# Seventeen attention blocks on GpSimd, and a shorter road for keys, queries, gate and output

## The chip, the cores and the metric

The kernel runs on one core of a Trainium2 chip. The core has five engines that work side by side and meet at semaphores: TensorE (PE, matrix products into PSUM), VectorE (DVE), ScalarE (ACT), GpSimd (POOL, which cannot reach PSUM) and SyncE (SP, which issues the transfers). The metric is the time on the device in microseconds (us). Each engine carries out its instructions in the order in which they stand in the program.

## The reference

Two attention layers over the same input x (2048 rows of 512, bf16) are mixed by a gate. Layer A is full attention over 32 heads of 16 columns. Layer B lets each position see eight earlier ones, two apart.

```
x = A_x
g = sigmoid((x * gate_w).sum(-1, keepdims=True))
a = softmax(q k^T * 16**-0.5) v  for 32 heads, then @ A_wo      # q, k, v = x @ A_wqkv
b = the same with B's weights, for keys at s, s-2, ..., s-14     # then @ B_wo
return g * a + (1 - g) * b
```

## The kernel before, in words

Layer A's scores are 32 heads x 16 tiles of 128 keys x 4 chunks of 512 queries: 2048 blocks of 128 keys by 512 queries. They are worked off in 32 periods; a period is one chunk of queries and one group of four heads (64 blocks). For a block PE multiplies a key tile and a query tile of 32 rows (a head's 16 rows and 16 rows for its bound), the exponential is taken, and PE multiplies the result by the values into one accumulator of the period (`pv_mm`); a column of constants beside the values gives the denominators.

The exponential of most blocks is ACT's: two PSUM rings, `rA` of three blocks and `rB` of two, take turns, and one ACT instruction does a ring's filling (`ex`, tile `pT`; the group pT<-ring). The others are DVE's, chosen per period by `n_dve`, 196 in all: `dq` on PE adds an offset (a matmul of `off` with the tile of ones) to the scores in a PSUM bank `misc`, and four DVE passes (`p1` to `p4`, tiles `dt` and `pd`) form the bits of a bf16 number that is the exponential.

Scores are kept in range by a bound. For each group of heads the largest absolute key entry is found (`km`, one pass over the projected keys; `kc` is a second pass that writes the keys and constant rows into `kt_all`), `selk` makes a row `rowq` of it, and the query tile `qt` carries absolute values of the query in its extra rows: `mg` masks the sign bits in PSUM and `ev` scales and writes. The first group's keys are written by ACT.

Layer B goes by tiles of 128 positions, one about every 47 us (`b_start`, `b_space`). Its keys and values are written to DRAM and read back shifted (`ksh`, `vsh`, eight shifts each); POOL multiplies and sums them (tile `prod`, two halves of logits and two of values), DVE and ACT do the small softmax, and `sm_div` multiplies by the reciprocal sums. POOL also scales A's transposed accumulators by the reciprocal denominators (`po2m`, tile `ott`).

The output of a tile is A's rows times A_wo (`a_part`), scaled by the gate on DVE (`a_ev`), and B's rows times B_wo (`b_part`), scaled by one minus the gate and added (`b_ev`). For the last two chunks the last group of heads comes separately (`tail`, `t_ev`). The gate goes through DRAM to be turned into one column per tile (`zfin`, `ztr`, `zsig`, `zgate`).

The order of all this is made when the program is built: every piece is an `Op` with an engine, a planned duration, a due time, its inputs and its buffers, and `list_schedule` places them on the engines. It also puts filler matmuls on zeros (`zero`) where PE would have too little to do. `CFG` holds planned durations, leads and the counts per period. The order on each engine is then fixed: at run time an instruction that waits holds all behind it on its engine. Nearly all instructions are issued by one helper line, so in the profile the tile names tell them apart.

At the start SP loads the four parts of x and the weights of A (x, keys, x, x, x, queries, values, 512 KB each), PE transposes x (`pxt`), and POOL and DVE copy each head's weights twice (`wtw`).

## Time and profile before

| | |
|---|---|
| median of three runs | 877.5 us (877.01 to 882.39) |
| profiled execution: its own time | 877.7 us |
| its span, first to last instruction | 875.9 us |
| mean granted clock of TensorE | 0.987 |
| busy: PE, DVE, ACT, POOL | 795.0, 735.4, 852.1, 619.3 us |
| first and last exponential of layer A | start 18.44, end 867.07 us |
| last work of layer B on POOL | end 788.7 us |
| data moved | 47.37 MB |

A row of the profile names the line, the engine and the operation, then the tiles (output <- inputs), the shapes and the count; behind the first bar are the busy time in us and the mean of one in ns, behind the second the engine's idle time just before these instructions and what ended it. A row of the timeline begins with the start and the duration, merged over instructions of one kind that follow one another.

### The profile page before, as it was taken

What the parts mean: (1) busy time and instruction counts of PE and PEld (TensorE: products, weight loads), DVE (VectorE), ACT (ScalarE), POOL (GpSimd) and SP (SyncE); (2) the same over time, 40 slices, a digit from 0 to 9 for tenths busy, and PEclk for the clock granted to TensorE, in tenths of its full rate; (3) what the DMA queues carried; (4) which work ended last, traced back from release to release, by engine and by line L of the source; (5) the groups of instructions that cost most, each with busy time, mean ns of one, the idle gap of its engine ahead of it and who ended that gap; (6) DMA issues with size and microseconds to landing.
All of it is one profiled execution on the core that took longest, in us unless ns stands there. A gap on an engine that the chain in (4) does not pass through costs nothing.

```text
span 875.9 us, 18559 instructions
## 1 busy us (share of the span) xinstructions
PE 795.0 (91%) x7468; PEld 257.9 (29%) x7468; DVE 735.4 (84%) x1217; ACT 852.1 (97%) x767; POOL 619.3 (71%) x607
## 2 busy tenths in 40 slices
PE   8999899999899999999899988899889889999885
PEld 4233233223322333223232322222222222322221
DVE  6488888898899788976869899988988998798996
ACT  5999999999999999999999999999999999999995
POOL 4176939696969779978996883979998959480000
PEclk9999999999999999999999999999999999999998
DMA  9301112103013103023120111121112031000001
GB/s 286 114 2 63 47 45 66 61 1 110 1 61 97 34 29 109 2 56 114 50 80 26 49 55 61 49 61 61 49 52 59 13 97 49 1 1 1 1 1 49
DMA packets 43998, 47.37 MB, mean 54 GB/s; under 512 B 1876, under 2 KB 41348, under 8 KB 43912
## 3 DMA queue, kind: packets, MB, share of 16 engines
q1 hardware_dynamic: 43912, 46.19, 16.6%
q8 instruction: 58, 0.95, 0.4%
q14 instruction: 28, 0.23, 0.1%
HBM read 39.86 MB, written 6.33 MB: 53 GB/s over the span
## 4 chain that ended last, share of the span: by engine, by line
ACT 66%; issue 25%; PE 7%; DVE 1%; DMA 1%; DVEq 0%; ACTq 0%
ACT pT L288 65%; PE misc_ps L300 3%; PE ring L300 2%; PE acc L300 2%; ACT lg L288 1%; DMA z_scr<-zrow 1%; PE pxt L496 1%; PE misc L300 0%; DVE zrow L288 0%; DVE osb L288 0%; ACT kt_all L288 0%; DVEq L1176 0%; DVE misc_ps L288 0%; DVE qt L288 0%; DVE accT L288 0%
## 5 line engine op out<-in xcount | busy, mean ns | idle before, releaser
L288 ACT ACTIVATE pT<-ring 128x1536 bf16<-128x1536 f32 x741 | 843.0, 1393 | 6.4 <-PE ring L300 6.1
L300 PE MATMUL ring<-qt,kt_all 32*128 32x512 bf16 x1852 | 295.9, 383 | 70.4 <-ACT pT L288 62.5
L288 POOL TENSOR_TENSOR prod<-prod 128x512 f32<-128x512 f32 (+1 forms) x208 | 240.0, 1169 | 6.3
L300 PE MATMUL acc<-pT,vp_all 128*17 128x512 bf16 (+1 forms) x1852 | 239.3, 387 | 1.0 <-ACT pT L288 0.7
L300 PEld LDWEIGHTS <-kt_all 32*128 32x128 bf16 x2048 | 119.1, 91 | 354.3 <-issue 334.8
L288 POOL TENSOR_TENSOR prod<-ksh,qb 128x512 f32<-128x512 bf16 x128 | 144.0, 1158 | 38.5 <-DMA ksh<-kv_scr 34.6
L288 DVE TENSOR_SCALAR dt<-misc 128x512 f32<-128x512 uint16 x196 | 133.9, 683 | 44.4 <-PE misc L300 42.6
L288 POOL TENSOR_TENSOR prod<-vsh,lg 128x512 f32<-128x512 bf16 x128 | 136.7, 1102 | 2.5 <-DMA vsh<-kv_scr 0.5
L288 DVE TENSOR_TENSOR dt<-misc,dt 128x512 f32<-128x512 uint16 x196 | 134.1, 684 | 4.8
L288 DVE SCALAR_TENSOR_TENSOR dt<-misc,dt 128x512 f32<-128x512 uint16 x196 | 134.2, 684 | 4.0
L288 DVE TENSOR_TENSOR pd<-misc,dt 128x512 uint16<-128x512 f32 x196 | 133.6, 681 | 2.8
L300 PEld LDWEIGHTS <-vp_all 128*17 128x17 bf16 (+1 forms) x2048 | 52.2, 88 | 127.5 <-issue 119.4
L300 PE MATMUL misc_ps<-xT,wtw 128*32 128x512 bf16 x1024 | 82.8, 384 | 0.0
L300 PE MATMUL misc<-ones_t,off 32*128 32x512 bf16 x196 | 74.9, 382 | 0.2 <-DVE osb L288 0.2
L300 PE MATMUL misc<-qt,kt_all 32*128 32x512 bf16 x196 | 73.8, 376 | 0.0
L300 PE MATMUL misc_ps<-bw,xT 128*32 128x512 bf16 x768 | 67.6, 391 | 0.0
L300 PE MATMUL acc<-ones_t,z 128*32 128x512 bf16 x179 | 63.7, 392 | 0.0
L288 POOL TENSOR_TENSOR ott<-accT,rden 128x256 bf16<-128x256 f32 x30 | 18.7, 623 | 57.1 <-DVE rden L288 57.1
L288 POOL TENSOR_TENSOR lg<-lg,mx 128x256 f32<-128x256 f32 x16 | 10.1, 631 | 48.4 <-DVE mx L288 48.4
L300 PEld LDWEIGHTS <-xT 128*32 128x32 bf16 (+1 forms) x1088 | 34.8, 96 | 28.8 <-issue 18.8
L300 PE MATMUL acc<-pd,vp_all 128*17 128x512 bf16 x196 | 42.3, 383 | 0.0
L288 POOL TENSOR_TENSOR lg<-lg,rr 128x256 f32<-128x256 f32 x16 | 10.1, 630 | 36.8 <-DVE rr L288 22.7
(73 smaller groups left out, 491.8 us busy)
## 6 DMA issues: line engine op xcount, KB each, us to landing
ksh<-kv_scr SPq DMA_DIRECT2D x16, 1024.0 KB, 6.0
vsh<-kv_scr SPq DMA_DIRECT2D x16, 1024.0 KB, 6.1
kv_scr<-kvs SPq DMA_DIRECT2D x16, 256.0 KB, 2.1
xld<-in_A_x_dram SPq DMA_DIRECT2D x4, 512.0 KB, 7.7
out_dram<-osb SPq DMA_DIRECT2D x16, 128.0 KB, 1.7
bw<-in_B_wqkv_dram SPq DMA_DIRECT2D x1, 1536.0 KB
wraw<-in_A_wqkv_dram SPq DMA_DIRECT2D x2, 512.0 KB, 8.7
wv<-in_A_wqkv_dram SPq DMA_DIRECT2D x1, 512.0 KB, 9.1
```

The costliest lines, as they stand in the source:

```text
L288: return chain_on(key, f(*a, **k))
L300: return chain(nc.tensor.matmul(out, lhsT=lhsT, rhs=rhs, start=start, stop=stop, **kw))
L496: chain(nc.tensor.transpose(out=st[half][:, c, tt * 128:(tt + 1) * 128], in_=xld[sc][:, tt, (2 * half + c) * 128:(2 * half + c + 1) * 128] ...
```

## The change

It has these parts:

- **Blocks.** The last key tiles' blocks go 202 to DVE and 17 to POOL (`n_dve`, `n_gp`). For a POOL block PE makes the scores as for DVE, DVE copies them to SBUF (into a `kvs` buffer), and POOL evaluates the same cubic in six passes (`gp_block`) with the `prod` buffer as scratch. ACT keeps 1829.
- **Keys.** For all groups but the first one DVE pass writes the projected keys and their maximum (both signs, since the extra rows hold the negated keys); `selk` joins the two, and four transfers then copy the constant rows over the extra rows from group 0.
- **Queries.** The scaling writes `qt` first, and the mask works on `qt` in SBUF, 32 bits at a time. The shift of the exponents moves into the bias of the exponential and into the offset.
- **Gate and output.** The gate is multiplied into A's reciprocal denominators and one minus the gate into B's reciprocal sums, both on POOL, so both products of an output tile are summed in one PSUM bank and DVE only copies.
- **Start.** x comes first, its first part in two halves; of the key and query weights the first four heads' columns come ahead, the rest last. Transposes go by pairs of row tiles, and DVE makes both of the first weight copies.
- **Ones.** The tile of ones shrinks to 128 columns, and matmuls that stream it read one column 512 times.
- The planning constants change. (In the first lines below they stand together; in the code each has its own line.)

```diff
-    n_dve=(3, 4, 5, 8, 4, 6, 5, 6, 7, 5, 5, 4, 6, 5, 5, 6, 8, 5, 7, 7, 7, 6, 8, 7, 7, 8, 7, 7, 8, 6, 7, 7),
-    dve_tiles=2,
+    n_dve=(4, 4, 8, 8, 3, 6, 5, 6, 5, 6, 6, 5, 5, 6, 8, 4, 9, 4, 6, 7, 7, 7, 7, 9, 6, 7, 9, 7, 7, 6, 7, 8),
+    n_gp=(1, 1, 1, 0, 0, 1, 0, 0, 0, 0, 0, 0, 1, 0, 1, 0, 0, 0, 0, 1, 1, 1, 0, 0, 0, 1, 0, 0, 2, 2, 1, 2),
+    gp_dl=8,
+    gp_lead=24,
+    dve_tiles=3,
...
-    d_slack=0.5, d_lead=4.0, dq_early=8.0, pd_bufs=5, same=3.0, early=0.25, a_slack=0.8, v_slack=0.3,
-    g_slack=2, unit=0.459, t0=18.5, b_start=30.0, b_space=46.7
+    d_slack=0.3, d_lead=3.0, dq_early=12.0, pd_bufs=4, same=3.5, early=0.3, a_slack=1.0, v_slack=0.1,
+    g_slack=3, unit=0.455, t0=17.0, b_start=32.0, b_space=47.1
...
+    def ones(rows):
+        b = ones_t[rows, 0:1]
+        return _ap(b, [list(b.ap[0]), [0, QW]])
...
+    o_x0 = load(load_x(0, 0, TPC // 2), alloc=[xtok[0]])
+    o_x[0] = load(load_x(0, TPC // 2, TPC), use=[xtok[0]])
+    o_wkh = load(load_w(1, 0, HC), alloc=[wtok])
+    o_x[1] = load(load_x(1), alloc=[xtok[1]])
+    o_x[2] = load(load_x(2), alloc=[xtok[2]])
+    o_x[3] = load(load_x(3), alloc=[xtok[3]])
+    o_wqh = load(load_w(0, 0, HC), use=[wtok])
+    o_wv = load(load_w(2))
+    o_wk = load(load_w(1, HC, D), use=[wtok])
+    o_wq = load(load_w(0, HC, D), use=[wtok])
     o_two = {}
-    o_two[1, 0] = op("dve", 0.72, twice(1, 0, 4), -6.0, deps=[o_wk], use=[wtok])
-    o_two[0, 0] = op("pool", 1.0, twice(0, 0, 4), -6.0, deps=[o_wq], use=[wtok], lat=1.3, slack=0.3)
-    o_two[1, 1] = op("pool", 5.0, twice(1, 4, H), -5.0, deps=[o_wk, o_two[0, 0]], use=[wtok], slack=1.0)
-    o_two[0, 1] = op("pool", 5.0, twice(0, 4, H), -4.0, deps=[o_two[1, 1]], use=[wtok], slack=1.0)
-    o_bw = op("sp", 1.0, load_bw, -8.3, lat=19.0)
+    o_two[1, 0] = op("dve", 0.45, twice(1, 0, 4), -6.0, deps=[o_wkh], use=[wtok])
+    o_two[0, 0] = op("dve", 0.45, twice(0, 0, 4), -5.9, deps=[o_wqh], use=[wtok])
+    o_two[1, 1] = op("pool", 3.6, twice(1, 4, H), -5.0, deps=[o_wk], use=[wtok], slack=1.0)
+    o_two[0, 1] = op("pool", 3.6, twice(0, 4, H), -4.0, deps=[o_wq], use=[wtok], slack=1.0)
...
-            V.tensor_scalar(out=kt_all[:, i, sc * QW:(sc + 1) * QW], in0=st["pk"][:], scalar1=rowc[:, 0:1],
-                            scalar2=rowc[:, 1:2], op0=ALU.mult, op1=ALU.add)
+            V.tensor_tensor_reduce(out=kt_all[:, i, sc * QW:(sc + 1) * QW], in0=st["pk"][:], in1=ones(slice(0, 128)),
+                                   scale=sign[:, 0:1], scalar=0.0, op0=ALU.mult, op1=ALU.max, accum_out=kmax_all[:, i, sc:sc + 1])
...
-        c = op("dve", 0.81, kc, dl - 0.8, deps=[b], use=[tk])
-        return op("dve", 0.70, km, dl, deps=[b, c], use=[tk])
+        return op("dve", 0.75, kc, dl, deps=[b, o_init_d], use=[tk])
...
+            if i == 0:
+                V.tensor_reduce(out=kmax[:, 0:1], in_=kmax_all[:, 0, :], axis=AX.X, op=ALU.max)
+            else:
+                V.tensor_reduce(out=kside[:, 0:1], in_=kmax_all[:, i, :], axis=AX.X, op=ALU.max)
+                V.stream_shuffle(out=kside[:, 1:2], in_=kside[:, 0:1], mask=[(p + DH) % 32 for p in range(32)])
+                V.tensor_tensor(out=kmax[:, i:i + 1], in0=kside[:, 0:1], in1=kside[:, 1:2], op=ALU.max)
...
+        def rows():
+            for j in range(4):
+                r_ = slice(32 * j + DH, 32 * j + 32)
+                SP.dma_start(out=kt_all[r_, i, :], in_=kt_all[r_, 0, :])
+        if i:
+            o_kc[i] = [op("sp", 2.2, rows, dl, deps=o_kc[i] + o_kc0, lat=6.0)] * NC
...
+        def ev():
+            V.tensor_scalar(out=qt_tiles[pi][:], in0=st["p1"][:], scalar1=rowq[:, i:i + 1], scalar2=None, op0=ALU.mult)
+
         def mg():
-            bits = st["p1"][:].bitcast(U32)
+            bits = qt_tiles[pi][:].bitcast(U32)
...
+        c = op("dve", 0.72, ev, dl - 0.8, deps=[b, o_selk[i]], use=[tk, tq])
+        o_q[pi] = op("dve", 0.35, mg, dl, deps=[c], use=[tq])
...
+    def zfin2():
+        st_g["zblk"] = work.tile([128, BPC, 32], FP32, name="zblk", tag="accT", bufs=2)
+        for j in range(4):
+            SP.dma_start(out=st_g["zblk"][32 * j:32 * j + 32, 0:2, :], in_=z_scr.rearrange("(h b p) -> b h p", b=32, p=32))
+
+    def zblk():
+        zb = st_g["zblk"][:, 0:2, :].rearrange("p h n -> p (h n)")
+        V.transpose(out=g_rows[:].rearrange("p h n -> p (h n)"), in_=zb)
+
+    def zblke():
+        A.activation(out=g_rows[:], in_=g_rows[:], func=ACT.Exp, scale=-1.0)
+
+    def zblkg():
+        V.tensor_scalar_add(out=g_rows[:], in0=g_rows[:], scalar1=1.0)
+        V.reciprocal(out=g_rows[:], in_=g_rows[:])
...
+            G.tensor_scalar(out=st["rr"][:], in0=st["rr"][:], scalar1=omg[:, t:t + 1], scalar2=None, op0=ALU.mult)
...
-            A.activation(out=st["p"][:, 0:n, :], in_=st["r"][:, 0:n, :], func=ACT.Exp, scale=LN2 / BITS)
+            A.activation(out=st["p"][:, 0:n, :], in_=st["r"][:, 0:n, :], func=ACT.Exp, scale=LN2 / BITS, bias=lift[:])
...
+        def gp_block(t, j, dl):
+            st = {}
+            tx, td, tp = tok("misc", NB), tok("kvs", 2), tok("pg", 2)
+
+            def dq():
+                st["x"] = ps.tile([128, QW], FP32, tag=f"misc{bank[0]}", bufs=1, name="misc")
+                st["xs"] = work.tile([128, 2 * D], BF16, name="kvs", tag="kvs", bufs=2)[:].bitcast(FP32)
+                row = slice(32 * j, 32 * j + 32)
+                mm(st["x"][:], off[row, :], ones(row), True, False, tile_position=(32 * j, 0))
+                mm(st["x"][:], kt_all[row, i, t * 128:(t + 1) * 128], qt_tiles[pi][row, :], False, True, tile_position=(32 * j, 0))
+
+            def cp():
+                V.tensor_copy(out=st["xs"], in_=st["x"][:])
+
+            def poly():
+                fr = st["xs"].bitcast(U16).rearrange("p (n two) -> p n two", two=2)[:, :, 0]
+                st["pd"] = work.tile([128, QW], BF16, name="pg", tag="pg", bufs=2)
+                prod = work.tile([128, WH, D], FP32, name="prod", tag="prod", bufs=1)
+                u, v = prod[:, 0, :], prod[:, 1, :]
+                G.tensor_scalar(out=u, in0=fr, scalar1=CUB_S, scalar2=None, op0=ALU.add)
+                G.tensor_tensor(out=v, in0=u, in1=u, op=ALU.mult)
+                G.tensor_scalar(out=v, in0=v, scalar1=EXP_C, scalar2=CUB_P, op0=ALU.mult, op1=ALU.add)
+                G.tensor_tensor(out=v, in0=v, in1=u, op=ALU.mult)
+                G.tensor_tensor(out=v, in0=v, in1=st["xs"], op=ALU.add)
+                G.tensor_scalar(out=st["pd"][:].bitcast(U16), in0=v, scalar1=CUB_Q, scalar2=None, op0=ALU.add)
+            a = op("pe", 0.43, dq, dl - 3.0 - cfg["gp_lead"], rows=True, deps=[o_q[pi], o_kc[i][t // TPC] if i else o_kc0[t // TPC]],
+                   alloc=[tx, td], use=[q_tok[pi]], rel=lo, lat=0.68, name=f"dq{pi}")
+            a = op("dve", 0.70, cp, dl - 2.0 - cfg["gp_lead"], deps=[a], use=[tx, td])
+            a = op("pool", 5.6, poly, dl - cfg["gp_dl"], deps=[a], alloc=[tp], use=[td], lat=5.9, slack=1.0, name=f"gp{pi}")
+            blocks.append((st, tp, a))
...
+            (gp_block if dorder.index((t, j)) >= n_dve[pi] else block)(t, j, hi - 1.0 - 3.5 * (n - 1 - q_))
...
+            E_ = V if pi >= NP - 2 else G
+            E_.tensor_tensor(out=rden[:], in0=rden[:], in1=g_rows[:, c_ // 2, (c_ % 2) * BPC:(c_ % 2 + 1) * BPC], op=ALU.mult)
...
+                    cols = slice(tt * 128, (tt + 1) * 128)
+                    if k < ng:
+                        mm_ct(st["pf"], oat_tiles[c_][:, k, cols], wop[:, k, :], k == 0, False)
+                    else:
+                        mm_ct(st["pf"], obt_tiles[c_][:, k - ng, cols], bwo[:, k - ng, :], False, k == ng + DC - 1)
...
+                V.tensor_copy(out=st["fa"], in_=st["pf"][:])
...
+                V.tensor_copy(out=st["o"][:], in_=st["pf"][:])
...
-                V.scalar_tensor_tensor(out=st["o"][:, 0:D], in0=st["pt"][:], scalar=g_sp[:, t:t + 1], in1=st["fa"],
-                                       op0=ALU.mult, op1=ALU.add)
+                V.tensor_tensor(out=st["o"][:, 0:D], in0=st["pt"][:], in1=st["fa"], op=ALU.add)
```

## The prediction

> **What bounds the kernel now.** I read the page's engine totals first, then the ScalarE (ACT) rows in order of time, then the clock row and the waits of GpSimd (POOL).
>
> ```profile
> PE 795.0 (91%) x7468; PEld 257.9 (29%) x7468; DVE 735.4 (84%) x1217; ACT 852.1 (97%) x767; POOL 619.3 (71%) x607
> ...
> L288 ACT ACTIVATE pT<-ring 128x1536 bf16<-128x1536 f32 x741 | 843.0, 1393 | 6.4 <-PE ring L300 6.1
> L300 PE MATMUL ring<-qt,kt_all 32*128 32x512 bf16 x1852 | 295.9, 383 | 70.4 <-ACT pT L288 62.5
> ```
>
> ACT is busy 97%, nearly all with one thing, the exponentials of 1852 score blocks; and it is TensorE (PE) that waits for ACT, 62.5 us, while ACT waits 6.1 us for PE. So the kernel is ACT's chain of exponentials, with something in front of it and something behind it. Those ends are in the timeline:
>
> ```profile
> 16.10 0.78 ACT L288 ACTIVATE kt_all<-misc_ps,rowc 128x512 bf16<-128x512 f32 x1 [0.52 <-DVE kmax_all L288]
> 18.44 6.88 ACT L288 ACTIVATE pT<-ring 128x1536 bf16<-128x1536 f32 x6 [1.56 <-PE ring L300]
> 25.71 1.45 ACT L288 ACTIVATE pT<-ring 128x1536 bf16<-128x1536 f32 x1 [0.39 <-PE ring L300]
> 27.52 14.71 ACT L288 ACTIVATE pT<-ring 128x1024 bf16<-128x1024 f32 x13 [0.36 <-PE ring L300]
> 43.59 4.62 ACT L288 ACTIVATE pT<-ring 128x1536 bf16<-128x1536 f32 x4 [1.35 <-PE ring L300]
> ```
> ```profile
> 849.09 17.98 ACT L288 ACTIVATE pT<-ring 128x1024 bf16<-128x1024 f32 x16
> ```
>
> The first exponential starts at 18.44. The last row is 16 of them back to back, eight of two blocks and eight of three: 40 blocks in 17.98 us, **0.4495 us per block**, ending at 867.07. The span is 875.9, so the tail is 8.8. Between 18.44 and 867.07 lie 848.6 us: 1852 x 0.4495 = 832.5, the 16 small softmax exponentials of block B 9.2, the gate's 0.2, and 6.7 lost. Of the lost time 4.5 stands in the bracketed waits of 0.36 to 1.35. Three of these waits (1.07 at 112.09, 0.57 at 376.02, 0.76 at 572.80) fall in the only stretches where the granted clock dips after the start (0.66 in 108 to 113, 0.56 and 0.76 in 368 to 378, 0.70 in 568 to 573); the 32x512 matmuls last 0.61 to 0.63 us there, elsewhere about 0.38. A dip costs ACT 0.8 us on average.
>
> **The change, part by part.**
>
> *Blocks off ACT.* VectorE (DVE) blocks go from 196 to 202, GpSimd gets 17: 1829 blocks stay on ACT, 23 fewer, 23 x 0.4495 = **10.3 us off the chain**. This counts in full as long as ACT stays the engine that everyone waits for. The exponential gets its bias from a tile in place of a constant: taken at nothing, since it reads a bias per partition either way.
>
> *What it puts on DVE.* Six blocks of four passes at 0.683: 6 x 4 x 0.683 = 16.4. Seventeen PSUM-to-SBUF copies for GpSimd, like the row that casts kvs (0.687): 11.7. Selecting a key bound gets a shuffle and a maximum on one column, near the 0.15 of the kmax row, seven times: 2.1. Gate rows and the second weight copy: 1.4. Together 31.6.
>
> *What it takes from DVE.* Keys and bounds in one pass: 28 x (0.804 + 0.681) become 28 of one pass with a second input and a maximum. No such instruction is in the trace; it costs between one 0.681 pass and the two passes it replaces, 1.485. I take 0.75, nearest the single-pass rows of this shape (0.681 to 0.804): 20.6 saved (bounds 0 to 22.5). The query mask moves from 512 words in PSUM (0.751) to 256 words in SBUF: between the 0.237 of a 16-wide SBUF reciprocal and 0.751, I take 0.4, the obt copy's 0.410: 32 x 0.35 = 11.2. The query scaling loses one of its scalars: 0.803 to 0.75, 1.7. Output: eight tiles drop 0.740 + 0.747 for one 0.687 copy, eight drop 0.751 + 0.750 for 0.69, and eight last sums 0.744 for 0.68: 6.4 + 6.5 + 0.5. Together 46.9. DVE's total falls by some 15 to 720 us, 83% of a shorter span; with the key pass at 1.485 it rises by 5. Neither makes it the bound.
>
> *GpSimd.* A block there is three two-input passes over 512 floats at 1.270 (row prod<-prod 128x512) and three one-input passes. One-input passes of that width are not in the trace: between 0.64, interpolated from the wtw copies (0.400 for 256 elements, 1.686 for 1792), and 1.270. I take 0.64, a one-input row: 5.7 us a block (upper bound 7.6), 97 for 17 (130). With 46 small multiplications at about 0.2 (between 0.10 for a one-column memset and 0.43 for 128 columns) POOL rises from 619 to some 725. Its windows: 76 of 80 us busy in 600 to 680, 56 to 71 in the other stretches between 40 and 760, and 20 of 108 after 760. The ten blocks of periods 0 to 25 add 57 us to about 590 in 740; the seven of periods 28 to 31 fall after 750, where POOL is nearly idle. So it fits on average.
>
> ```profile
> POOL ott L288 <- DVE rden L288: 57.1, 7, 25.4
> POOL lg L288 <- DVE mx L288: 48.4, 6, 10.4
> POOL prod L288 <- DMA ksh<-kv_scr: 34.6, 4, 19.8
> ```
>
> These are the places where POOL waits for others today, 140 us in all, and can absorb work.
>
> *PE.* A block taken off ACT needs one more matmul (the offset): 23 x 0.38 at most, 9 us, beside 62.5 of ring waits and 64 of filler matmuls. The offset and filler matmuls now read one repeated column of ones. No row shows such an operand; they run at 0.382 and 0.392, and the slowest row of this width, in the cold clock, is 0.63: bounds 0 to 0.25 on about 400 matmuls. I take 0, since the existing rows hardly differ with what is streamed (0.376 to 0.395).
>
> *SP and DMA.* Each head group but the first gets four transfers of 64 KB that restore the constant key rows, 28 issues in all, in SP's order between block B's loads. Issues take 0.3 to 1.0 and a 256 KB store of kvs lands in 2.1, the eight 64 KB wop loads in 8.5 beside other loads. The first scores of a group now wait for them. Behind a waiting `rows` transfer on SP stand the ksh and vsh loads and the stores; their reader is POOL, then far later the output. It is due some 19 us before its period, so I take nothing; if that cover is gone, the lateness comes on ACT once per group, seven times.
>
> *Start.* Today the sixth 512 KB load (wq) is ready at 12.55 and the first (x) at 5.01: 1.5 us each, so x's last part comes at about 11.0. In the new order a 64 KB slice of wk takes the place of all of wk ahead of it, so it comes between 9.7 and 11.0 (the slice's short rows could cost as much as the full load). From there, by rows: transposes 1.07, copy 1.01, key projection 1.05, bound 0.69, selection 0.45, query scaling 0.75, mask 0.4, scores and the first exponential 0.5, with semaphore gaps some 6.2. From PE's start at 10.4 that is 16.6, 1.9 earlier than 18.44. Bounds: 0.3 (only the mask's share: 0.6 us of it stands ahead of the selection today) to 2.2. I take **1.6**, for a slice that is a little slow.
>
> *Tail.* One multiplication of 0.2 is added in front of the last transposes; four final sums drop from 0.744 to 0.68. **0.** The new gate-row exponential is 0.2 on ACT.
>
> *Sum.* 875.9 - 10.3 - 1.6 + 0.2 = 864.2, with the 6.7 lost on ACT kept. The profiled execution took 877.7 for a span of 875.9, so 866.0; its time is 0.2 above the median of the runs shown, 877.5, so **865.8**.
>
> **A rule weighed.** The moved mask is one-source, SBUF to SBUF. The nearest DVE row of that kind beside a busy POOL, the oat transpose, lasts 698 to 711 ns at all 16 occurrences, so no blocking shows there. The Trainium skill, "SBUF — State Buffer", Who interferes with whom, says that such an operation in a two-port mode and a GpSimd instruction block each other wholly; it names scalar operations for it and not transposes, so no run here shows it. By it the mask would wait out a POOL instruction.
>
> **The rivals.**
>
> 1. *ACT's waits go.* For: DVE is relieved and the order is new. Against: the start and the clock dips made most of them. With 1 us left of 6.7 and the best start: 859.5. Chance 12%.
>
> 2. *More waits on ACT*, from clock dips or late key rows: at 0.8 a dip, or seven late groups at 1 us, 5 to 10 us: 869 to 876. For: three dips exist now with the fillers. Against: PE's load hardly changes. 10%.
>
> 3. *The mask waits for GpSimd.* POOL is busy about 76% of 40 to 760 in pieces of about 1.2 us, so a blocked mask waits 0.76 x 0.6 = 0.46 on average, at most 1.27. If this reached ACT in full, 32 x 0.46 = 15 us: 881; if half, 873. Against: the mask runs well ahead of its period, and DVE has 140 us of idle time. It eats the whole gain from 0.37 us per mask. 7%. (The skill's rule above is the ground for it.)
>
> 4. *GpSimd becomes the gate: slower.* The PV matmul of a GpSimd block sits in PE's fixed order, and behind it stand the score matmuls of ACT's ring; the block's input buffer is shared with block B's kvs, so a late one also holds DVE. POOL runs passes of block B in stretches of 9.3 us (4.50 + 4.51 + 0.43), and a block that falls behind one comes that much late. The place is periods 12 and 25 (about 335 to 361 and 673 to 699) and their neighbours, where POOL shows no idle. Against: the waits above, and a planned lead of 8 us. Price: 17 blocks x L, less about 1 us of ring. The gain of 11.7 is gone at 0.7 us of stall per block; at 1.2 it is 20 us: 886. 9%.
>
> 5. *The change doesn't do what it says*: x is not earlier, only 0.3 gained: 867.1. This lies inside the forecast's own spread of 861 to 868.5, which has 62%.
>
> **How the numbers follow.** Forecast 62%, rivals 12, 10, 7 and 9. One per cent, 8.8 us, is about what a measurement can tell from no change here: 868.7 and 886.3 are the marks. Faster: 62 + 12 + 1 = 75. Within: the rest of case 2, nearly all of case 3 and some of 4: 17. Slower: 8. The range from 859.5 to 876 leaves out half of case 1, about half of case 3 and case 4.
>
> **What would show it.** ACT's exponential group with 1829 blocks' worth (732 instructions, some 833 busy) and its waits still under 10; first exponential at 16.3 to 17.2; POOL near 725 busy with block passes of 0.6 and 1.27; DVE near 720, the key pass at 0.75; a tail of 8.8. Wrong it would be if ACT's waits grew past 15, with POOL as what PE waits for at a pd or pg matmul, or with many slices of a lower clock.

## The result and the profile after

The change made the kernel slower: 960.55 us, the median of four runs (955.19 to 963.11), against 877.26 for the kernel before. The ratio is 1.093 (95% interval 1.086 to 1.099), where 865.8 had been forecast. (Medians and ranges are over all runs of a kernel; ratios and their intervals leave out single runs in a slower state.) The profiled execution took 955.19 for a span of 953.0, 77.1 more than the span of before.

The page of the kernel after, its totals, its clock row and its first two groups:

```profile
PE 840.3 (88%) x7436; PEld 267.5 (28%) x7436; DVE 737.4 (77%) x1271; ACT 909.7 (95%) x759; POOL 754.4 (79%) x753
...
PEclk9999899997999999979999978879879979977998
...
L293 ACT ACTIVATE pT<-ring,lift 128x1536 bf16<-128x1536 f32 x732 | 900.0, 1452 | 22.2 <-PE ring L309 18.6
L309 PE MATMUL ring<-qt,kt_all 32*128 32x512 bf16 x1829 | 308.7, 402 | 98.9 <-ACT pT L293 81.9
```

ACT still carries the time, and PE waits for it more than before (81.9 us, before 62.5). The group of exponentials has 732 instructions, nine fewer than before, as the change says; yet it is busy for 900.0 us where it was 843.0. So the busy time per instruction grew, from 843.0 / 741 = 1.138 us to 900.0 / 732 = 1.230. ACT also stands idle longer in front of them (22.2 against 6.4, of which 18.6 and 6.1 are waits for PE's ring), and the clock row, which before was nines but for its last slice, has many sevens and eights.

The timeline of ACT in the kernel after (start, duration, then what the rows merge):

```profile
16.38 1.01 ACT L293 COPY xT<-pxt 128x1024 bf16<-128x1024 bf16 x1 [1.36 <-DVE xT L293]
...
21.49 35.66 ACT L293 ACTIVATE pT<-ring,lift 128x1536 bf16<-128x1536 f32 x29 [1.44 <-PE ring L309]
...
288.31 55.06 ACT L293 ACTIVATE pT<-ring,lift 128x1024 bf16<-128x1024 f32 x45
...
440.99 48.92 ACT L293 ACTIVATE pT<-ring,lift 128x1024 bf16<-128x1024 f32 x40
...
892.63 51.08 ACT L293 ACTIVATE pT<-ring,lift 128x1536 bf16<-128x1536 f32 x42 [0.18 <-PE ring L309]
```

The first exponential starts at 21.49 and not at 16.8; before it was 18.44. The last ends at 943.71, which leaves a tail of 9.3 (before 8.8). So of the 77.1 us more, 3.05 are at the start, 0.5 in the tail, and 73.6 in the stretch of exponentials (922.2 against 848.6), although that stretch holds 23 blocks fewer, worth 10.3. Some 84 us have to be found there.

### The profile page after: what moved, and what is told of

Same layout as the page of the kernel before. It is cut to its first block, busy times and chain, and to the rows that moved or that the text cites. A ratio compares the mean times of both kernels' runs of the same rounds, so it can differ in the third digit from the quotient of the medians.

```text
span 953.0 us, 18737 instructions
## 1 busy us (share of the span) xinstructions
PE 840.3 (88%) x7436; PEld 267.5 (28%) x7436; DVE 737.4 (77%) x1271; ACT 909.7 (95%) x759; POOL 754.4 (79%) x753
## 3 DMA queue, kind: packets, MB, share of 16 engines
q1 hardware_dynamic: 46200, 48.06, 16.6%
## 4 chain that ended last, share of the span: by engine, by line
ACT 54%; issue 28%; PE 17%; DVE 1%; DVEq 0%; ACTq 0%
ACT pT L293 53%; PE acc L309 6%; PE ring L309 5%; PE misc_ps L309 3%; PE misc L309 2%; ACT lg L293 1%; PE pxt L523 1%; DVE accT L293 0%; ACT xT L293 0%; DVE xT L293 0%; DVE wtw L293 0%; DVE qt L293 0%; PE misc_ps L919 0%; DVEq L1261 0%; DVE oat L293 0%
## 5 line engine op out<-in xcount | busy, mean ns | idle before, releaser
L293 ACT ACTIVATE pT<-ring,lift 128x1536 bf16<-128x1536 f32 x732 | 900.0, 1452 | 22.2 <-PE ring L309 18.6
L309 PE MATMUL ring<-qt,kt_all 32*128 32x512 bf16 x1829 | 308.7, 402 | 98.9 <-ACT pT L293 81.9
L293 POOL TENSOR_TENSOR prod<-prod 128x512 f32<-128x512 f32 (+1 forms) x242 | 279.5, 1167 | 9.1
L309 PE MATMUL acc<-pT,vp_all 128*17 128x512 bf16 (+1 forms) x1829 | 247.6, 407 | 1.5 <-ACT pT L293 0.5
L309 PEld LDWEIGHTS <-kt_all 32*128 32x128 bf16 x2048 | 126.4, 92 | 402.2 <-issue 370.6
L309 PE MATMUL misc<-ones_t,off 32*128 32x512 bf16 x219 | 87.5, 401 | 0.6 <-DVE pd L293 0.4
L309 PE MATMUL misc<-qt,kt_all 32*128 32x512 bf16 x219 | 87.0, 399 | 0.1
L309 PE MATMUL acc<-ones_t,z 128*32 128x512 bf16 x135 | 55.7, 451 | 0.0
L293 POOL TENSOR_SCALAR prod<-kvs 128x512 f32<-128x512 uint16 x17 | 25.4, 1494 | 33.3 <-DVE kvs L293 32.3
L309 PEld LDWEIGHTS <-wtw 128*32 128x32 bf16 x1024 | 26.1, 97 | 31.6 <-issue 19.0
```

Of the source, the lines that this page charges most:

```text
L293: return chain_on(key, f(*a, **k))
L309: return chain(nc.tensor.matmul(out, lhsT=lhsT, rhs=rhs, start=start, stop=stop, **kw))
```

## The experiments

Each experiment ran beside the kernel before on the same chip (medians 877.5 to 879.5), and ratios are against those runs. The labels stand for the kernels; "the constant-bias kernel" is e1_imm, which most of the others start from.

### The bias of the exponential (e1_imm, e2_before_tilebias)

e1_imm is the kernel after with one operand changed:

```diff
-            A.activation(out=st["p"][:, 0:n, :], in_=st["r"][:, 0:n, :], func=ACT.Exp, scale=LN2 / BITS, bias=lift[:])
+            A.activation(out=st["p"][:, 0:n, :], in_=st["r"][:, 0:n, :], func=ACT.Exp, scale=LN2 / BITS, bias=LIFT * LN2)
```

> The changed kernel with one edit: the bias of the ring's exponentials is the same number as a constant in the instruction, not a tile. Same order on every engine, same output. Theory A (a bias read from a tile costs ACT about 0.1 us per instruction): in the changed kernel 85 to 112 blocks in stretches without a wait take 0.489 us each, before 0.4495; 732 instructions x 0.0993 = 73 us come back, and with the faster ACT the TensorE clock dips less, so ACT's waits fall from some 18 us toward 7: 870 to 882 us. Theory B (the GpSimd blocks or the new waits hold up PE, ACT is slow because its ring is late): the time stays above 930.

e2_before_tilebias is the kernel before with a zero bias that comes from a tile:

```diff
+    zbias = const.tile([128, 1], FP32, name="zbias")
...
+        V.memset(zbias[:], 0.0)
...
-            A.activation(out=st["p"][:, 0:n, :], in_=st["r"][:, 0:n, :], func=ACT.Exp, scale=LN2 / BITS)
+            A.activation(out=st["p"][:, 0:n, :], in_=st["r"][:, 0:n, :], func=ACT.Exp, scale=LN2 / BITS, bias=zbias[:])
```

> The kernel before with one edit: the ring's exponentials take their bias (zero) from a tile of 128 zeros instead of the constant zero. Theory A: 741 x 0.0993 = 74 us more, and the clock dips come as in the changed kernel (some 5 to 15 us more waits): 950 to 968 us, mean clock near 0.93. Theory B: within 1 per cent of 877.

Measured: e1_imm 890.34 us (883.36 to 892.88, ten runs), ratio 1.011 (1.007 to 1.015), 70.2 below the kernel after. e2_before_tilebias 956.05 us, ratio 1.084 (1.075 to 1.093), 78.1 above the kernel before. One operand takes most of the regression away and, put alone into the kernel before, makes one as large. Its row on the page of e2_before_tilebias:

```profile
L288 ACT ACTIVATE pT<-ring,zbias 128x1536 bf16<-128x1536 f32 x741 | 910.4, 1504 | 17.2 <-PE ring L300 15.7
```

Against the row of before, 67.4 more are busy time (843.0) and 10.8 more are idle time in front of the instructions (6.4): 78.2 of the 78.5 by which the span grew (954.4 against 875.9).

The order of e1_imm's instructions is that of the kernel after, so its timeline of ACT has the same two long stretches as shown above:

```profile
18.32 33.31 ACT L293 ACTIVATE pT<-ring 128x1536 bf16<-128x1536 f32 x29 [1.56 <-PE ring L309]
...
267.55 50.95 ACT L293 ACTIVATE pT<-ring 128x1024 bf16<-128x1024 f32 x45
...
406.33 45.52 ACT L293 ACTIVATE pT<-ring 128x1024 bf16<-128x1024 f32 x40
```

The 45 exponentials last 55.06 with the tile and 50.95 with the constant: 4.11 / 45 = 0.091 us each. The 40 last 48.92 and 45.52: 0.085 each. The other pair of kernels says the same. First the row of e2_before_tilebias, then the matching one of the kernel before:

```profile
47.89 24.50 ACT L288 ACTIVATE pT<-ring,zbias 128x1536 bf16<-128x1536 f32 x20
```
```profile
48.14 22.75 ACT L288 ACTIVATE pT<-ring 128x1536 bf16<-128x1536 f32 x20
```

1.75 / 20 = 0.0875 each. (The page names the tile as an input only where one is read: ring,lift and ring,zbias against ring.) The Trainium skill, "ScalarE: Activation LUTs", What ACT_TABLE_LOAD costs, states about 93 ns for each such operand of a column per partition, and the trace agrees: 0.085 to 0.091 in these rows, 0.081 in the first row of each timeline (35.66 against 33.31 for 29). By form, the mean of a two-block exponential rises by 0.084 (1.157 to 1.241) and that of a three-block one by 0.086 (1.578 to 1.664), so the price goes by the instruction and not by the block. For 732 of them it is 65.8 by the groups' busy times (900.0 against 834.2). Of the 71.8 between the two profiled executions (955.19 and 883.36), 3.2 more lie at the start and 2.2 in ACT's waits.

The page of e1_imm, its clock row and the same two groups:

```profile
PEclk9999899999999999999999978999999999979998
...
L293 ACT ACTIVATE pT<-ring 128x1536 bf16<-128x1536 f32 x732 | 834.2, 1367 | 20.0 <-PE ring L309 16.2
L309 PE MATMUL ring<-qt,kt_all 32*128 32x512 bf16 x1829 | 296.3, 388 | 58.8 <-ACT pT L293 51.8
```

Most of the sevens and eights are gone: with the tile bias alone the mean clock of the kernel before falls too, from 0.985 to 0.954 (means over the runs). With the longer exponential PE waits longer for the ring (97.8 in e2_before_tilebias against 62.5), and the granted clock falls with it.

What remains is smaller, and the rest of the runs is about it. e1_imm is 12.4 above the kernel before, where the prediction had 11.7 below, and outside the 870 to 882 expected of it. Its profiled execution (883.36, the fastest of its ten runs) is 5.3 longer in span than that of before: 10.3 less for the blocks, nothing at the start (18.32 against 18.44), 0.2 more in the tail, and 15.5 more lost on ACT. That loss comes out as before: the stretch from 18.32 to 872.13 is 853.8; 1829 x 0.4495 = 822.1 and 9.5 for the small exponentials leave 22.2, where the kernel before left 6.7. The page agrees by another road: the idle time in front of the exponentials is 20.0 against 6.4.

### The start (e3_imm_warm, e4_imm_copy, e8_imm_halves)

In the kernel after, the second pair of weight copies stands beside GpSimd's large copies, which begin at 13.99. The timeline of DVE in the kernel after:

```profile
6.25 0.35 DVE L293 COPY wtw<-wraw 128x256 bf16<-128x256 bf16 x2
...
13.90 1.85 DVE L293 COPY wtw<-wraw 128x256 bf16<-128x256 bf16 x2
```

Two copies of one shape take 0.35 beside an idle GpSimd and 1.85 beside a busy one. Besides, ACT's copies of x wait for DVE's (the row of 16.38 above, 1.36), since both read one PSUM tile, and PE's first 16 projections last 0.63 each where they last 0.38 in e1_imm (the profile lists a granted clock of 1.00 in both). Three kernels take these one at a time. e3_imm_warm runs more warming matmuls ahead of the first transposes:

```diff
-        for _ in range(6):
+        for _ in range(9):
```

> As e1_imm, with 36 warm-up matmuls ahead of the transposes instead of 24 (before: 32). In the changed kernel 16 transposes of the start take 0.31 us each and the first projection 1.90 us for 16 matmuls, before 0.22 and 1.05. If the short warm-up leaves the array at half speed, the first exponential moves from 21.5 to about 18.5 to 19.5 and the time falls by 2 to 3 us against e1_imm. If the new order of loads and copies is what is late, it stays at 21 or later.

e4_imm_copy holds GpSimd's copies until DVE's are done:

```diff
-    o_two[1, 1] = op("pool", 3.6, twice(1, 4, H), -5.0, deps=[o_wk], use=[wtok], slack=1.0)
+    o_two[1, 1] = op("pool", 3.6, twice(1, 4, H), -5.0, deps=[o_wk, o_two[0, 0]], use=[wtok], slack=1.0)
```

> As e1_imm, with GpSimd's large weight copies held until VectorE's small copy of the query weights is done. In the changed kernel that small copy takes 1.85 us while GpSimd copies, its twin for the keys 0.35 us while GpSimd is idle. If the two engines lock each other out, the copy falls to about 0.35 to 0.5 us and the first exponential comes up to 1.4 us earlier (20.1), unless another link of the start is late anyway: then it stays at 21.5.

e8_imm_halves gives the halves that ACT and DVE copy a PSUM tile each, as in the kernel before, and gets a new order from the plan:

```diff
-                if half == 0:
-                    pxt = ps.tile([128, 2, 2, QW], BF16, tag=tag, bufs=1, name="pxt")
-                    st[0], st[1] = pxt[:, 0], pxt[:, 1]
...
+                st[half] = ps.tile([128, 2, QW], BF16, tag=tag, bufs=1, name="pxt")
```

> As e1_imm, with the transposed x of each quarter in two PSUM tiles as before, one for ACT's copy and one for VectorE's, in place of one tile for both; loads and weights stay in the new order. In the changed kernel each of ACT's four copies waits until VectorE's copy of the same tile is done (5.4 us in e1, 7.8 in the changed kernel), before they ran side by side. If that is what cost the start its gain: the first exponential at 16.5 to 17.5 in place of 18.3 to 21.5, and 1 to 3 us less time. If the cold array clock is: no earlier than 18.

Measured: e3_imm_warm 892.59 (two runs), first exponential at 19.67; e4_imm_copy 889.15 (ratio 1.009, 1.004 to 1.014), first exponential at 19.55; e8_imm_halves 899.31 (ratio 1.019), first exponential at 19.98. None gained more than its runs scatter. In e8_imm_halves ACT no longer waits for DVE's half. In e4_imm_copy the hold never came into play: the copy, 0.36 long, stood at 10.94, and GpSimd's copies began at 13.99, when their weights had arrived. e1_imm's own profile has the copy at 0.36 too, with nothing done about it, so the 1.85 in the kernel after comes of a start as late as 13.90.

Another link was late in place of those aimed at. In e3_imm_warm it is the warming itself: the first transposes start at 5.00 and not at 3.72. In e4_imm_copy it is the first query mask, which runs beside GpSimd's weight copies (13.99 to 20.60). First two rows of e1_imm, then the same two of e4_imm_copy:

```profile
17.35 0.48 DVE L293 TENSOR_SCALAR qt<-qt,magn 128x256 uint32<-128x256 uint32 x1
...
17.88 0.60 PE L309 MATMUL ring<-qt,kt_all 32*128 32x512 bf16 x5 [0.95 <-DVE qt L293]
```
```profile
17.27 1.79 DVE L293 TENSOR_SCALAR qt<-qt,magn 128x256 uint32<-128x256 uint32 x1
...
19.11 0.60 PE L309 MATMUL ring<-qt,kt_all 32*128 32x512 bf16 x5 [2.26 <-DVE qt L293]
```

The mask takes 1.31 more, the scores behind it start 1.23 later, and so does the first exponential. At this one place the waiting mask of rival 3 reaches ACT.

Between profiles of kernels with one order of instructions the first exponential moves from 18.0 to 21.5. So the start varies by some 3 us from run to run, none of the profiles has it before 18.0, and which link is last is not fixed. No one cause holds for all of them.

### GpSimd (e12_imm_gpshort, e5_imm_gp72, e6_imm_nogp)

The prediction's fourth rival was a late GpSimd block that holds PE. It is there in e1_imm; in the kernel after, whose exponentials are slower, the list of PE's waits has none for pg. The timeline of e1_imm around 782 us:

```profile
780.47 1.49 POOL L293 TENSOR_SCALAR pg<-prod 128x512 uint16<-128x512 f32 x1
...
782.01 0.58 PE L309 MATMUL acc<-pg,vp_all 128*17 128x512 bf16 x1 [3.36 <-POOL pg L293]
...
782.96 0.61 PE L309 MATMUL ring<-qt,kt_all 32*128 32x512 bf16 x2
...
783.66 1.02 ACT L293 ACTIVATE pT<-ring 128x1024 bf16<-128x1024 f32 x1 [3.19 <-PE ring L309]
```

GpSimd finishes the block at 781.96; PE had waited 3.36 for it, with the ring's score matmuls behind it, and ACT in turn 3.19. PE then works in a low clock (granted 0.50 from 782 to 790; 0.61 for a matmul that else takes 0.38) and ACT waits three times more, 0.48, 1.34 and 0.47. In the list of waits of e1_imm there are four such, and 6.6 us in all:

```profile
PE ring L309 <- ACT pT L293: 51.8, 185, 0.7
...
ACT pT L293 <- PE ring L309: 16.2, 16, 3.2
...
PE acc L309 <- POOL pg L293: 6.6, 4, 3.4
```

A block takes longer than the plan's 5.6. The groups by form of POOL in the kernel after (count, busy, mean ns):

```profile
L293 POOL TENSOR_TENSOR prod<-prod 128x512 f32<-128x512 f32 x210 | 259.8, 1251 | 6.6
...
L293 POOL TENSOR_SCALAR pg<-prod 128x512 uint16<-128x512 f32 x17 | 25.6, 1505 | 1.5
L293 POOL TENSOR_SCALAR prod<-kvs 128x512 f32<-128x512 uint16 x17 | 25.4, 1494 | 33.3 <-DVE kvs L293 32.3
L293 POOL TENSOR_TENSOR prod<-prod,kvs 128x512 f32<-128x512 f32 x17 | 21.6, 1270 | 1.3
...
L293 POOL TENSOR_SCALAR prod<-prod 128x512 f32<-128x512 f32 x17 | 10.6, 621 | 1.5
```

Of the three one-input passes, the one on floats costs 0.621, and the two that read or write 16-bit integers cost 1.49 and 1.51, more than a two-input pass. (The one that reads them takes every second 16-bit word; which part that has in its time was not tried.) Together 2 x 1.251 + 1.505 + 1.494 + 1.270 + 0.621 = 7.4 us.

e12_imm_gpshort keeps the order and shortens the blocks by leaving out the cubic's correction, so these 17 get a coarser exponential:

```diff
-                G.tensor_scalar(out=u, in0=fr, scalar1=CUB_S, scalar2=None, op0=ALU.add)
-                G.tensor_tensor(out=v, in0=u, in1=u, op=ALU.mult)
-                G.tensor_scalar(out=v, in0=v, scalar1=EXP_C, scalar2=CUB_P, op0=ALU.mult, op1=ALU.add)
-                G.tensor_tensor(out=v, in0=v, in1=u, op=ALU.mult)
-                G.tensor_tensor(out=v, in0=v, in1=st["xs"], op=ALU.add)
-                G.tensor_scalar(out=st["pd"][:].bitcast(U16), in0=v, scalar1=CUB_Q, scalar2=None, op0=ALU.add)
+                G.tensor_scalar(out=u, in0=fr, scalar1=0.0, scalar2=None, op0=ALU.mult)
+                G.tensor_tensor(out=v, in0=u, in1=st["xs"], op=ALU.add)
+                G.tensor_scalar(out=st["pd"][:].bitcast(U16), in0=v, scalar1=0.0, scalar2=None, op0=ALU.add)
```

> As e1_imm, in the same order on PE, DVE and ACT, with three of the six GpSimd passes of a block left out (the cubic's correction; the 17 blocks get a coarser exponential): about 4.3 us a block in place of 7.4. If the late GpSimd blocks cost what PE's waits for pg suggest: these waits vanish, and with the dips that follow them 4 to 9 us go: 881 to 886. If the time stays within 3 us of e1, they are not what separates 890 from 878.

e5_imm_gp72 tells the plan the measured length instead, and e6_imm_nogp gives the 17 blocks back to ACT; both get a new order from the plan:

```diff
-            a = op("pool", 5.6, poly, dl - cfg["gp_dl"], deps=[a], alloc=[tp], use=[td], lat=5.9, slack=1.0, name=f"gp{pi}")
+            a = op("pool", 7.2, poly, dl - cfg["gp_dl"], deps=[a], alloc=[tp], use=[td], lat=7.5, slack=1.0, name=f"gp{pi}")
```

> As e1_imm, with the planned duration of a GpSimd block 7.2 us in place of 5.6 (its availability at 7.5 in place of 5.9), so that the order written out reckons with what six passes took: 1.49, 1.25, 0.62, 1.27, 1.27, 1.50, about 7.4 in all. In e1 PE waits 6.6 us in four places for a GpSimd block, and ACT's two longest waits (2.00 at 600, 3.19 at 783, the latter with 2.3 more in the 8 us behind it) follow two of them. If the short plan is the cause: PE's waits for pg under 2 us, and 4 to 8 us less than e1 (median 890): 880 to 887. If the clock dips are what costs: within 3 us of e1.

```diff
-    n_gp=(1, 1, 1, 0, 0, 1, 0, 0, 0, 0, 0, 0, 1, 0, 1, 0, 0, 0, 0, 1, 1, 1, 0, 0, 0, 1, 0, 0, 2, 2, 1, 2),
+    n_gp=(0,) * 32,
```

> As e1_imm, with no block on GpSimd: its 17 go to ACT (1846 blocks). ACT's work rises by 17 x 0.4495 = 7.6 us, DVE loses 17 copies (11.7), GpSimd 127. If the GpSimd blocks are worth what was forecast: 7 to 9 us more than e1, 897 to 899. If their waits and the crowding they bring to PE's order eat that: within 3 us of e1 or below it.

Measured: e12_imm_gpshort 883.64 (ratio 1.0065, 1.003 to 1.010), and PE's waits for pg are gone from its list; ACT's waits for PE's ring fell by only 1.5, from 16.2 to 14.7. e5_imm_gp72 905.53 (ratio 1.032), e6_imm_nogp 893.65 (ratio 1.015). With the order kept, short blocks gain 6.7 by the medians and 4.2 by the ratios of the two kernels to the kernel before; their intervals overlap. The plan with true lengths freed PE of pg (0.9 us left) and was 15 slower, with new stalls elsewhere. The timeline of ACT in e5_imm_gp72:

```profile
777.80 9.14 ACT L293 ACTIVATE pT<-ring 128x1024 bf16<-128x1024 f32 x8 [4.12 <-PE ring L309]
792.68 27.23 ACT L293 ACTIVATE pT<-ring 128x1024 bf16<-128x1024 f32 x24 [5.74 <-PE acc L309]
...
885.22 2.36 ACT L293 ACTIVATE pT<-ring 128x1536 bf16<-128x1536 f32 x2 [8.67 <-PE acc L309]
```

So GpSimd's lateness is real in e1_imm and costs a few microseconds at most, not the 12.4. That e6_imm_nogp is 3 above e1_imm shows no worth of the 17 blocks either way, as its order is another one.

### The column of ones (e11_imm_ones, e16_imm_ones_gpshort)

e11_imm_ones reads 256 real columns of ones twice where the kernel after reads one column 512 times, in PE's matmuls only and with the same order; e16_imm_ones_gpshort joins this and the short GpSimd blocks:

```diff
-        return _ap(b, [list(b.ap[0]), [0, QW]])
+        return _ap(b, [list(b.ap[0]), [0, 2], [1, QW // 2]])
...
-    ones_t = const.tile([128, 128], BF16, name="ones_t")
+    ones_t = const.tile([128, QW // 2], BF16, name="ones_t")
```

> As e1_imm, with the offset, filler and warm-up matmuls streaming 256 real columns of ones twice, in place of one column 512 times; PE's order is the same to the instruction. If the repeated column costs nothing, as forecast: within 3 us of e1 (890) and the same clock. If it makes PE count as less busy and lets the clock fall: clock near 0.985, 876 to 882.

> e11 and e12 together, in e1's order on PE, DVE and ACT: real columns of ones, and three of six GpSimd passes left out (a coarser exponential in 17 blocks). If the two effects add: 878 to 882, the kernel before within 1 per cent. If both runs only fell on kinder stretches of the clock: 884 to 890.

Measured: e11_imm_ones 886.34 (ratio 1.010, 1.007 to 1.013), against e1_imm's 1.011: no difference that these intervals tell apart. Its offset matmuls last 388 ns on average, those of e1_imm 383, those of before 382; no cost of the repeated column shows. e16_imm_ones_gpshort 884.0 (ratio 1.008): the sum of the two "gains" is not there. Its profiled execution lost 849.3 - 822.1 - 9.5 = 17.7 on ACT, still 11 more than the kernel before.

### The clock and the fillers (e7_imm_cover, e15_imm_fill2)

e1_imm's mean clock is 0.958 over its runs, that of the kernel before 0.985. If the low clock were the cause, more filler matmuls should mend it. e7_imm_cover asks the plan for more cover; e15_imm_fill2 keeps the order and doubles each filler (135 become 270):

```diff
-    cover=0.68,
+    cover=0.76,
```

> As e1_imm, with the planner's floor for PE's work in any 3.4 us raised from 0.68 to 0.76, which adds filler matmuls. In e1 the granted clock is 0.972 on average (0.987 before) and ACT's waits, 20 us in all, stand mostly in the stretches of low clock. If too little PE work is what lets the clock fall: clock above 0.985, ACT's waits near 10, 878 to 884. If the fillers get in the way of the ring's scores, or the dips come from stalls that fillers don't cover: clock unchanged, 888 or more.

```diff
-        for _ in range(n if spots else 0):
+        for _ in range(2 * n if spots else 0):
```

> As e1_imm, with two filler matmuls wherever the plan has one in the accumulators, and no other instruction moved. If the low clock follows from too little PE work and costs ACT its waits: clock above 0.97 and 880 to 886. If the fillers take PE time that the ring's scores need: clock up or not, 890 or more.

Measured: e7_imm_cover 901.38 (ratio 1.025, 1.022 to 1.028; a new order) at a clock of 0.976, e15_imm_fill2 889.24 (ratio 1.014, 1.009 to 1.018) at 0.971. The page of e15_imm_fill2:

```profile
PEclk9999999899999999999999979999999999998998
...
L293 ACT ACTIVATE pT<-ring 128x1536 bf16<-128x1536 f32 x732 | 836.2, 1325 | 21.8 <-PE ring L309 18.7
...
L309 PE MATMUL acc<-ones_t,z 128*32 128x512 bf16 x270 | 80.9, 405 | 0.0
```

The clock rose about half of the way to the 0.985 of before, the idle time in front of the exponentials did not fall (21.8 against 20.0) and the time stayed. More fillers raise the clock, but that alone does not take the stalls away.

Still, the time goes with the clock from run to run. In the 48 runs of the kernel before that stand beside the experiments it goes from 874.17 us at a clock of 0.994 to 888.55 at 0.968. At the same clocks e1_imm is not slower: 889.03 at 0.968 and 883.36 at 0.972, where the kernel before took 888.55 and 886.96. So what is left of the loss comes together with a lower clock: the order of e1_imm gets the lower one as a rule, that of before only now and then. Whether the stalls bring the clock down or the clock brings the stalls is not shown.

### The written order (e9_before_consts, e10_imm_beforeconsts, e13_before_t0, e14_imm_t0)

The order of the instructions comes out of planned durations. e9_before_consts gives the kernel before only the new planning constants, e10_imm_beforeconsts the constant-bias kernel the old ones (the lines stand together here; in the code each has its own):

```diff
-    d_slack=0.5, d_lead=4.0, dq_early=8.0, pd_bufs=5, same=3.0, early=0.25, a_slack=0.8, v_slack=0.3,
-    g_slack=2, unit=0.459, t0=18.5, b_start=30.0, b_space=46.7
+    d_slack=0.3, d_lead=3.0, dq_early=12.0, pd_bufs=4, same=3.5, early=0.3, a_slack=1.0, v_slack=0.1,
+    g_slack=3, unit=0.455, t0=17.0, b_start=32.0, b_space=47.1
```

(e10_imm_beforeconsts is this reversed, without pd_bufs.)

> The kernel before with the new planning constants alone (slacks, leads, unit, t0, b_start, b_space, pd_bufs; the counts of blocks and all code as before): the order on every engine is planned anew. If the written order, and not any part of the computation, costs what is left of the loss (890 in e1 against 878): 885 to 895, with clock below 0.975 and ACT waits of 15 us or more. If a part of the change costs it: 874 to 882.

> As e1_imm, with the planning constants of the kernel before (all but pd_bufs, for which SBUF has no room): the parts of the change in an order planned with other slacks. If any order that wasn't fitted to these durations loses some 10 us: 888 to 905. If the new constants are what costs: 870 to 880.

e13_before_t0 and e14_imm_t0 are controls. They move the planned start of the first period by 0.1 us, which means nothing for the work, but makes the plan anew:

```diff
-    t0=18.5,
+    t0=18.6,
```

> The kernel before with one planning number moved by 0.1 us (t0 from 18.5 to 18.6), which plans the order anew and means nothing for the work. If an order as good as the one before is the rule: 875 to 880. If the order before is a rare fit and any other loses, as the 896 with all new constants suggests: 882 to 897.

```diff
-    t0=17.0,
+    t0=17.1,
```

> As e1_imm, with t0 from 17.0 to 17.1, the same meaningless step on the changed kernel: if the order decides, anywhere from 882 to 902 (e1: 890); if the parts of the change do, 887 to 893.

Measured: e9_before_consts 896.05 (ratio 1.016, 1.010 to 1.023), e10_imm_beforeconsts 899.61 (1.024), e13_before_t0 887.82 (1.0105, 1.006 to 1.015), e14_imm_t0 912.88 (1.040, 1.035 to 1.044). The meaningless 0.1 us costs the kernel before 10 us and e1_imm 22.5. In e14_imm_t0 the order happens to put a GpSimd block later still against PE:

```profile
848.79 0.58 PE L309 MATMUL acc<-pg,vp_all 128*17 128x512 bf16 x1 [4.08 <-POOL pg L293]
...
850.02 1.02 ACT L293 ACTIVATE pT<-ring 128x1024 bf16<-128x1024 f32 x1 [4.25 <-PE ring L309]
```

In e13_before_t0 nothing of the change is there, and ACT is idle 15.3 in front of its exponentials where it is 6.4 in the kernel before:

```profile
L288 ACT ACTIVATE pT<-ring 128x1536 bf16<-128x1536 f32 x741 | 844.0, 1382 | 15.3 <-PE ring L300 14.1
```

All newly planned orders of both kernels, with the bias a constant, lie between 887.8 and 912.9 us. The 877 of the kernel before is the exception among the orders that ran, with its 6.7 lost on ACT; e1_imm's 890 is one of the better ones.

## Why the prediction was wrong

**The failed step** is the last sentence on the blocks off ACT: "The exponential gets its bias from a tile in place of a constant: taken at nothing, since it reads a bias per partition either way". It does not read one either way. The trace of before names only the ring as input of its 741 exponentials, while the key rows in the same list name their tile (kt_all<-misc_ps,rowc); both were read. The operand costs 0.08 to 0.09 us per instruction on the one engine that bounds the kernel, 66 us on 732 of them; e1_imm and e2_before_tilebias show it from both sides (70 less, 78 more, with what follows in waits, clock and start). No bound was set and no rival spoke of it: an edit of one operand was passed over because it looks like no work. The page of the Trainium skill named above has this price; the prediction did not draw on it.

**"The 6.7 lost on ACT kept"** was the term that was mis-sized in what remains. It measured 22.2 in the profiled execution of e1_imm, the fastest of ten. A new order does not inherit the waits of the old one. Rival 2 (more waits on ACT) had this direction with at most 10 us and 10%. How much of the 12.4 belongs to the parts of the change and how much to the order that it happened to get stays open: the controls move by 10 and 22, so no part can be credited with less than that through a newly planned kernel. Within one order, GpSimd's lateness is worth at most some 2 to 7 (e16_imm_ones_gpshort against e11_imm_ones 2.3, e12_imm_gpshort against e1_imm 6.7, both with overlapping intervals) and the ones nothing that shows.

**The start** was worth 1.6 in the sum, between bounds of 0.3 and 2.2. It gained nothing that holds: 18.0 to 21.8 for the first exponential in the profiles of the constant-bias kernels, 18.44 before. The chain of rows summed to 16.6 with copies that do not wait for one another; the copies that share a PSUM tile, and the weight copies and the first mask beside GpSimd, were not priced.

**What held.** ACT stays the bound, with 732 instructions. By the groups' busy times the 23 blocks take 8.8 off it (843.0 to 834.2 with the bias constant), by the rate of the unbroken rows the 10.3 of the forecast. The tail is 9.1 to 9.3 for 8.8. DVE's sum comes out with three corrections; the groups by form of DVE in the kernel after:

```profile
L293 DVE CUSTOM_DVE_ANT_0 kt_all<-misc_ps,ones_t,sign 128x512 bf16<-128x512 f32 x28 | 20.9, 748 | 13.9 <-PE misc_ps L309 13.5 <-PE acc L309 0.3
L293 DVE TENSOR_SCALAR qt<-qt,magn 128x256 uint32<-128x256 uint32 x32 | 19.7, 615 | 0.4
...
L293 DVE TENSOR_TENSOR kmax<-kside 128x1 f32<-128x1 f32 x7 | 3.4, 492 | 0.2
...
L293 DVE DVE_READ_ACCUMULATOR2_ANT kmax_all<- 128x1 f32 x28 | 2.3, 82 | 0.0
```

The key pass is 0.748, as chosen (0.75), with a read of its accumulator of 0.082 that was not foreseen. The mask is 0.615 where 0.4 was taken, and the maximum on one column 0.492 where 0.15 was. In e1_imm (mask 0.653, maximum 0.582) these add 32 x 0.253 + 7 x 0.43 + 2.3 = 13.4 to the forecast 720; it measured 732.1. POOL was forecast at 725 with one-input passes of 0.64; the two on 16-bit integers add 17 x (0.865 + 0.854) = 29.2, and it measured 754.4. The block of 7.4 lies within the upper bound of 7.6. The rows' transfers on SP, taken at nothing, show in no wait of PE for kt_all, in e1_imm or in the kernel after.

**The rivals.** Rival 3 had the mechanism and not the price: a mask alone takes 0.35 (at 20.64 in the kernel after, where GpSimd's last copy had ended at 20.54), 0.615 to 0.653 on average, so it waits about 0.3 for GpSimd, some 9 us in all. DVE has that idle, but for the first mask, on which the first exponential waits: PE's waits for qt come to 4.0 us in e1_imm. The rule of the Trainium skill weighed there ("SBUF — State Buffer", Who interferes with whom) is borne out by these masks, 0.31 to 1.38 long in the kernel after, by the first one of 1.79 in e4_imm_copy and by the copies of 0.35 and 1.85, beside GpSimd copies of 1.68 each. Rival 4, GpSimd as the gate, has its stalls in e1_imm at four places and 6.6 us, and not the 0.7 per block that decide; the kernel after has none. The sign that the prediction named, ACT's waits past 15 with POOL as what PE waits for at a pg matmul, is seen in e1_imm; it was not what made the change slow.

No version that ran beats the kernel before. The nearest that does all the work is e11_imm_ones at 886.34.

## What to carry to other kernels

Price every operand of the instruction that the bounding engine issues most: a scalar that moves from a constant into a tile looks free, and its few hundredths of a microsecond are multiplied by the count. An order written out from planned durations is a fit to one kernel: where any edit makes it anew, first measure what a meaningless nudge of the plan does, and credit no part with less than that. What two engines lose to a shared path is read from the same instruction with and without the neighbour, and it matters only where the loser has no idle time.

## What the runs showed of the hardware

- A bias read from a tile makes an exponential of 128x1024 or 128x1536 longer by 0.08 to 0.09 us, with zeros in the tile as with another value.
- On GpSimd a one-input pass over 512 elements takes 0.62 us from float to float, and 1.49 to 1.51 where it reads (every second word) or writes 16-bit integers.
- On DVE, SBUF-to-SBUF operations lengthen beside GpSimd: two copies from 0.35 to 1.85, a mask of 256 words from 0.35 to 0.62 on average and 1.79 at most in the rows shown. A maximum of two single columns in SBUF averages 0.49 to 0.58; a reduction of four columns to one takes 0.15.
- More fillers raised the granted clock (0.958 to 0.971 in one order, 0.976 in another) without shortening the kernel.
- One kernel, unchanged, takes 874.17 us in a run with a mean granted clock of 0.994 and 888.55 in one of 0.968.
